# Folding a block-diagonal matrix into a projection by 32 by 32 tiles of the TensorE array

## The chip, the cores and the metric

The kernel runs on one core of one Trainium2 chip. The metric is the device time of one execution in microseconds (us). The kernel before takes 1632.44 us (median of 3 runs, 1632.38 to 1632.49). PE is the tensor engine's matmul stream, PEld its weight loads, DVE the vector engine, ACT the scalar engine, SP the queue that issues most transfers.

## The reference, cut to what matters

Four blocks run in turn on x of 2048 by 1024: attention, gated linear unit, and both again. Only attention is concerned:

```python
H = 32; Dh = D // H                       # 32 heads of 32
q, k, v = split(layernorm(x) @ wqkv)
phi = lambda t: jnp.where(t > 0, t + 1, jnp.exp(t)) + 1e-6
pq, pk = phi(q), phi(k)
kv  = einsum("bhsd,bhse->bhde", pk, v)    # one 32 by 32 matrix per head
num = einsum("bhqd,bhde->bhqe", pq, kv)
den = einsum("bhqd,bhd->bhq", pq, pk.sum(s)) + 1e-6
x = x + (num / den) @ wo
```

As (pq kv) wo = pq (kv wo), the kernel multiplies each head's 32 by 32 matrix into its 32 rows of wo once ("the fold", whose result is T) and then does one dense product per 128 tokens.

## The kernel before: the parts that matter

kv comes out as 128 by 128 blocks for four heads each. Only the four diagonal 32 by 32 pieces are wanted; a mask zeroes the others, and the fold is a full matmul per block and half of wo's columns:

```python
# head of the program: a mask with ones in the diagonal blocks, five memsets on DVE
for b in range(H):                                   # finish_kv: H = 2 here
    nc.vector.tensor_tensor(out=kvT[...], in0=kv[b]..., in1=self.mask..., op=ALU.mult)
...
def fold_wo(i):                                      # i = 0..15
    n2, g = divmod(i, G)
    ps = pool.tile([P, NW], F32, tag=tag)            # one of four PSUM banks
    nc.tensor.matmul(ps, lhsT=kvT[:, g, :], rhs=ring.get((l, f"o{n2}"))[:, g, :],
                     start=True, stop=True)
    # copied to T by ACT (odd g) or DVE (even g)
...
# two folds after each of eight units of eight matmuls
```

The head of the program issues ten warm-up matmuls on zeros, which wait for one DVE memset queued behind those of the mask.

## Time and profile before

| what | before | how to read it |
|---|---|---|
| time, median | 1632.44 us | device time of one execution |
| span of the profiled run | 1631.2 us | first to last instruction |
| PE busy | 1625.2 us | nearly all of the span |
| full folds | 32 | 16 in each of two attention layers |
| projections (L403) | 1024 | the order in which these read is changed too |

Busy times of PE rest on modelled ends of matmuls, so prices of matmuls below are taken from start to start where they can be; the length of a group in a timeline includes the modelled end of its last matmul. In the rows of a timeline the columns are start, length in us, engine, line, operation, output and inputs, shape, count, and in brackets idle time of the engine before it with what ended it.

### The profile page before, as it was taken

How to read it: one execution, taken by the hardware profiler on the slowest of the kernel's cores; microseconds unless marked ns; L12 is line 12 of the kernel's file. 1: busy time of each engine (PE TensorE's matmuls, PEld its weight loads, DVE VectorE, ACT ScalarE, POOL GpSimd, SP SyncE). 2: the span in 40 equal slices, each digit the busy share in tenths (PEclk: the TensorE clock that was granted, in tenths of full speed). 3: DMA queues.
4: the chain of work that ended last, by engine and by line, in shares of the span. 5: the costliest groups of instructions: out<-in, count | busy, mean ns of one | idle time of the engine just before them, and what ended most of it. 6: DMA issues, size and time to landing. Idle time of an engine off the chain costs nothing.

```text
span 1631.2 us, 18462 instructions
## 1 busy us (share of the span) xinstructions
PE 1625.2 (100%) x7658; PEld 743.1 (46%) x7658; DVE 570.8 (35%) x947; ACT 331.2 (20%) x636; POOL 201.5 (12%) x134
## 2 busy tenths in 40 slices
PE   9999999999999999999999999999999999999999
PEld 4444444444444444444444444444444444444444
DVE  7855695113212222222264547941022111211211
ACT  6741212101110110111066312121011101101110
POOL 2349220000000000000023592100000000000000
PEclk9999999999999999999999999999999999999999
DMA  8313637448445445544550147464554454454452
GB/s 248 62 52 59 175 71 201 145 151 232 155 145 188 160 150 162 168 151 138 166 124 1 52 98 244 84 193 145 179 166 149 156 186 155 145 165 155 155 161 72
DMA packets 298245, 235.05 MB, mean 144 GB/s; under 512 B 101296, under 2 KB 294192, under 8 KB 298160
## 3 DMA queue, kind: packets, MB, share of 16 engines
q1 hardware_dynamic: 292832, 228.75, 47.5%
q10 hardware_dynamic: 5328, 5.11, 0.9%
q8 instruction: 60, 0.98, 0.2%
q14 instruction: 25, 0.20, 0.0%
HBM read 201.33 MB, written 8.39 MB: 129 GB/s over the span
## 4 chain that ended last, share of the span: by engine, by line
PE 98%; ACT 1%; DMA 0%; DVE 0%; issue 0%; SPq 0%
PE pu L628 24%; PE pg L628 24%; PE acc L652 23%; PE ps L403 12%; PE ps L520 7%; PE ps L437 7%; DMA t<-in_A_wqkv_dram 0%; PE kv L450 0%; PE fold L508 0%; PE acc_last L652 0%; ACT e L355 0%; ACT e L354 0%; ACT e L356 0%; PE tp L264 0%; DVE pq L362 0%
## 5 line engine op out<-in xcount | busy, mean ns | idle before, releaser
L628 PEld LDWEIGHTS <-t 128*128 128x128 bf16 x3584 | 350.7, 98 | 422.8
L628 PE MATMUL pu<-xnT,t 128*128 128x512 bf16 x1792 | 423.3, 379 | 0.0
L628 PE MATMUL pg<-xnT,t 128*128 128x512 bf16 x1792 | 423.3, 379 | 0.0
L652 PE MATMUL acc<-t,hT 128*128 128x512 bf16 x1764 | 382.5, 379 | 0.0
L634 DVE TENSOR_TENSOR hT<-pu,rg 128x512 bf16<-128x512 f32 x224 | 154.6, 690 | 572.9 <-PE pu L628 572.9
L633 ACT ACTIVATE rg<-pg 128x512 f32<-128x512 f32 x224 | 133.5, 596 | 737.4 <-PE pg L628 737.4
L652 PEld LDWEIGHTS <-hT 128*128 128x128 bf16 x1820 | 178.1, 98 | 209.0
L403 PE MATMUL ps<-t,xnT 128*128 128x512 bf16 x1024 | 224.7, 379 | 1.0 <-DMA t<-in_A_wqkv_dram 0.6
L403 PEld LDWEIGHTS <-xnT 128*128 128x128 bf16 x1024 | 99.8, 98 | 121.2 <-issue 1.8
L520 PE MATMUL ps<-T,pqT 128*128 128x512 bf16 x512 | 111.8, 379 | 0.0
L149 ACT ACTIVATE rstd<-mv,eps 128x1 f32<-128x1 f32 x64 | 18.7, 293 | 327.8 <-DVE mv L147 327.7
L669 DVE TENSOR_TENSOR xo<-x,acc 128x512 bf16<-128x512 f32 x31 | 21.3, 688 | 170.3 <-PE acc L652 170.3
L483 POOL TENSOR_TENSOR prod<-pq,zrow 128x1024 f32<-128x1024 bf16 x32 | 67.9, 2123 | 87.8 <-DVE den L488 75.6
L142 DVE BATCH_NORM_STATS2 stats<-x 128x6 f32<-128x512 f32 (+1 forms) x120 | 77.9, 672 | 0.8
L520 PEld LDWEIGHTS <-pqT 128*128 128x128 bf16 x512 | 50.1, 98 | 60.4
L417 POOL CAST ksum<-x 128x512 f32<-128x512 bf16 x2 | 1.7, 866 | 605.4 <-DVE x L362 605.4
L666 DVE TENSOR_TENSOR x<-x,acc 128x512 f32<-128x512 f32 x32 | 21.6, 674 | 138.5 <-PE acc L652 137.4
L419 POOL TENSOR_TENSOR ksum<-ksum,slab 128x512 f32<-128x512 f32 x46 | 53.6, 1171 | 86.3 <-DVE slab L362 76.8
L362 DVE SCALAR_TENSOR_TENSOR pq<-ps,e 128x512 bf16<-128x512 f32 x64 | 44.0, 688 | 55.7 <-ACT e L356 55.2
L495 POOL TENSOR_TENSOR pq<-pq,den 128x1024 bf16<-128x1024 bf16 x32 | 61.7, 1933 | 3.1 <-DVE den L490 3.1
L488 DVE TENSOR_REDUCE den<-prod 128x32 f32<-128x1024 f32 x32 | 38.9, 1217 | 52.6 <-POOL prod L483 52.6
L437 PE MATMUL ps<-slab,x 128*128 128x512 bf16 x256 | 56.6, 379 | 0.0
(58 smaller groups left out, 609.0 us busy)
## 6 DMA issues: line engine op xcount, KB each, us to landing
t<-in_B_W_gate_dram SPq DMA_DIRECT2D x56, 1024.0 KB, 7.0
t<-in_B_W_up_dram SPq DMA_DIRECT2D x56, 1024.0 KB, 5.4
t<-in_B_W_down_dram SPq DMA_DIRECT2D x64, 896.0 KB, 5.0
t<-in_A_wqkv_dram SPq DMA_DIRECT2D x11, 1024.0 KB, 6.2
t<-in_A_wo_dram SPq DMA_DIRECT2D x4, 1024.0 KB, 6.8
away<-x SPq DMA_DIRECT2D x8, 512.0 KB, 4.1
x<-away SPq DMA_DIRECT2D x8, 512.0 KB, 7.8
out_dram<-xo ACTq DMA_DIRECT2D x31, 128.0 KB, 2.3
```

Source lines behind the costliest of these rows:

```text
L142: self.nc.vector.bn_stats(out=stats[:, c, :], in_=src[:, c * fmax:(c + 1) * fmax])
L362: nc.vector.scalar_tensor_tensor(out=out, in0=ps, scalar=0.0, in1=e, op0=ALU.max, op1=ALU.add)
L403: nc.tensor.matmul(ps, lhsT=self.xnT[l, l_q][:, kt, j * P:(j + 1) * P], rhs=w[:, kt, :], start=(kt == 0), stop=(kt == KT - 1))
L419: nc.gpsimd.tensor_tensor(out=ksum[:, cols], in0=ksum[:, cols], in1=pk, op=ALU.add)
L437: nc.tensor.matmul(ps, lhsT=self.xn[l, t][:, d * P:(d + 1) * P], rhs=self.pk[l, t][:, h * NW:(h + 1) * NW], start=(t == 0), stop=(t == sel ...
L483: nc.gpsimd.tensor_tensor(out=prod, in0=pq_of[sc, j], in1=zrow, op=ALU.mult)
L495: nc.gpsimd.tensor_tensor(out=heads(pq), in0=heads(pq), in1=den[:, :].unsqueeze(2).to_broadcast([P, D // HD, HD]), op=ALU.mult)
L520: nc.tensor.matmul(ps, lhsT=pqT[sc][:, g, j * P:(j + 1) * P], rhs=T[g // 2][:, g % 2, n2 * NW:(n2 + 1) * NW], start=(g == 0), stop=(g == G ...
L628: nc.tensor.matmul(ps, lhsT=w[:, kt, fi * P:(fi + 1) * P], rhs=self.xnT[l, q][:, kt, :], start=(kt == 0), stop=(kt == KT - 1))
L633: nc.scalar.activation(out=rg, in_=pg, func=ACT.Relu)
L634: nc.vector.tensor_tensor(out=h[:, fi, :], in0=pu, in1=rg, op=ALU.mult)
L652: nc.tensor.matmul(ps[:, 0:n], lhsT=hT[ft // 4][:, ft % 4, j * P:(j + 1) * P], rhs=wd[:, k, i * n:(i + 1) * n], start=(ft == 0), stop=(ft ...
```

## The change

The intent is to spend no array rows on zeros. Each head's 32 by 32 matrix becomes the weights of one tile of the array, so sixteen heads fill it. For this, sixteen heads need sixteen different places (row group by column group), so the heads of keys and queries are put in another order when the projection reads its weights. The mask goes away. The diff, cut to its core:

```diff
-        self.mask = ...                       # and its five memsets
+        R = P // HD
+        by_row = lambda a: a.rearrange("p (i b d) -> p i b d", i=R, d=HD)
 # projections of k and q
-    nc.tensor.matmul(ps, lhsT=..., rhs=w[:, kt, :], ...)
+    nc.tensor.matmul(by_row(ps), lhsT=..., rhs=w[:, kt, :].rearrange("p (b i d) -> p i b d", ...), ...)
 # kv
-    rhs=mt[:, g * P:(g + 1) * P]
+    rhs=by_row(mt[:, b * NW:(b + 1) * NW])[:, :, i, :]
 # finish_kv: two masked products on DVE
+    nc.vector.tensor_copy(out=kvT[first half], in_=kv[0])
+    nc.scalar.activation(out=kvT[second half], in_=kv[1], func=ACT.Copy)
 # fold: four bursts of sixteen tiles in place of sixteen full matmuls
+    for b in range(R):
+        g = a * R + b
+        for i in range(R):
+            e = slice(i * HD, (i + 1) * HD)
+            nc.tensor.matmul(ps[i][b * HD:(b + 1) * HD, :], lhsT=kvT[e, g, e],
+                             rhs=wo[e, g, :], start=True, stop=True,
+                             tile_position=(i * HD, b * HD))
 # a burst after every second unit, starting one unit earlier
```

More of the change, by code (lines that the diff above doesn't have):

```diff
@@ L124, in __init__ @@
         nc.vector.memset(self.ones, 1.0)
-        self.mask = self.const.tile([P, P], F32, name="mask")
-        nc.vector.memset(self.mask, 0.0)
-        for i in range(P // HD):
-            nc.vector.memset(self.mask[i * HD:(i + 1) * HD, i * HD:(i + 1) * HD], 1.0)
         self.eps6 = self.const.tile([P, 1], F32, name="eps6")
@@ L402, in project @@
                     between()
-                nc.tensor.matmul(ps, lhsT=self.xnT[l, l_q][:, kt, j * P:(j + 1) * P],
-                                 rhs=w[:, kt, :], start=(kt == 0), stop=(kt == KT - 1))
+                nc.tensor.matmul(by_row(ps), lhsT=self.xnT[l, l_q][:, kt, j * P:(j + 1) * P],
+                                 rhs=w[:, kt, :].rearrange("p (b i d) -> p i b d", i=R, d=HD),
+                                 start=(kt == 0), stop=(kt == KT - 1))
             return ps
@@ L449, in kv_step @@
                 b, i = divmod(g, NW // P)
-                nc.tensor.matmul(kv[b][:, i * P:(i + 1) * P],
+                nc.tensor.matmul(kv[b][:, i * P:(i + 1) * P].rearrange("p (i d) -> p i d", d=HD),
                                  lhsT=ring.get((l, f"v{b}"))[:, d, i * P:(i + 1) * P],
-                                 rhs=mt[:, g * P:(g + 1) * P], start=(d == 0 and i == 0),
+                                 rhs=by_row(mt[:, b * NW:(b + 1) * NW])[:, :, i, :], start=(d == 0 and i == 0),
                                  stop=(d == KT - 1 and i == NW // P - 1),
@@ L460, in finish_kv @@
             n = NW // P
-            for b in range(H):
-                nc.vector.tensor_tensor(out=kvT[:, b * n:(b + 1) * n, :],
-                                        in0=kv[b][:, :].rearrange("p (g e) -> p g e", e=P),
-                                        in1=self.mask[:, :].unsqueeze(1).to_broadcast([P, n, P]),
-                                        op=ALU.mult)
+            nc.vector.tensor_copy(out=kvT[:, 0:n, :].rearrange("p g e -> p (g e)"), in_=kv[0])
+            nc.scalar.activation(out=kvT[:, n:2 * n, :].rearrange("p g e -> p (g e)"), in_=kv[1],
+                                 func=ACT.Copy)
         def q_unit(sc, j, c, lag=None):
@@ L500, in z_scale, with fold_wo @@
             nc.sync.dma_start_transpose(out=pqT[sc][:, :, j * P:(j + 1) * P], in_=pq)
-        def fold_wo(i):
-            n2, g = divmod(i, G)
-            if n2 == 0 and g % 2 == 0:
-                T.append(self.slab.tile([P, 2, D], BF16, tag="slab", name=f"T{l}_{g // 2}"))
-            pool, tag = (self.kvp, f"kv{g // 2 % 2}") if g % 2 else (self.ps3, "b")
-            ps = pool.tile([P, NW], F32, tag=tag, name=f"fold{l}_{i}")
-            nc.tensor.matmul(ps, lhsT=kvT[:, g, :], rhs=ring.get((l, f"o{n2}"))[:, g, :],
-                             start=True, stop=True)
-            dst = T[g // 2][:, g % 2, n2 * NW:(n2 + 1) * NW]
-            if g % 2:
-                nc.scalar.activation(out=dst, in_=ps, func=ACT.Copy)
-            else:
-                nc.vector.tensor_copy(out=dst, in_=ps)
+        def fold_wo(n):
+            n2, a = divmod(n, H)
+            if n2 == 0:
+                T.extend(self.slab.tile([P, 2, D], BF16, tag="slab", name=f"T{l}_{2 * a + i}")
+                         for i in range(2))
+            ps = [pool.tile([P, NW], F32, tag=tag, name=f"fold{l}_{n}_{i}") for i, (pool, tag) in
+                  enumerate(((self.kvp, "kv0"), (self.kvp, "kv1"), (self.ps3, "b"), (self.ps3, "b")))]
+            wo = ring.get((l, f"o{n2}"))
+            for b in range(R):
[5 more added lines that the diff above has]
+                                     tile_position=(i * HD, b * HD))
+            for i in range(R):
+                g = a * R + i
+                dst = T[g // 2][:, g % 2, n2 * NW:(n2 + 1) * NW]
+                if g % 2:
+                    nc.scalar.activation(out=dst, in_=ps[i], func=ACT.Copy)
+                else:
+                    nc.vector.tensor_copy(out=dst, in_=ps[i])
         def out_unit(sc, j, n2):
@@ L585, in with_fold @@
             def with_fold(u, i):
-                return lambda: (u(), fold_wo(2 * i), fold_wo(2 * i + 1))
-            run(q3[:3])
-            run([with_fold(u, i) for i, u in enumerate(q3[3:] + out0[:3])])
+                return lambda: (u(), fold_wo(i // 2) if i % 2 == 0 else None)
+            run(q3[:2])
+            run([with_fold(u, i) for i, u in enumerate(q3[2:] + out0[:1])])
+            run(out0[1:3])
             ring.free_slowly((l, "o0"), later, 2)
```

## The prediction

> **What bounds the kernel now.** I read the page first: busy shares, then the chain that ended last. It says that the tensor engine is the whole story.
>
> ```profile
> PE 1625.2 (100%) x7658; PEld 743.1 (46%) x7658; DVE 570.8 (35%) x947; ACT 331.2 (20%) x636; POOL 201.5 (12%) x134
> PE 98%; ACT 1%; DMA 0%; DVE 0%; issue 0%; SPq 0%
> PE pu L628 24%; PE pg L628 24%; PE acc L652 23%; PE ps L403 12%; PE ps L520 7%; PE ps L437 7%; DMA t<-in_A_wqkv_dram 0%; PE kv L450 0%; PE fold L508 0%; PE acc_last L652 0%; ACT e L355 0%; ACT e L354 0%; ACT e L356 0%; PE tp L264 0%; DVE pq L362 0%
> ```
>
> PE is busy for 1625.2 of 1631.2 us and holds 98% of the chain. So only two things move the time: PE's own work, and a wait that the change makes PE take. Work on DVE, ACT or the queues is free as long as PE does not stand for it. The fold is under half a per cent of the chain, so a large move could only come from something else that the change touches.
>
> Next the view of the tile that the change rewrites (the fold), with its count and durations, and the page's row of the projections, whose addressing is changed as well:
>
> ```profile
> L508 PE MATMUL fold<-t,kvT x32: 379/379/380, 173.6 to 997.6; 128*128 128x512 bf16 x32
> L512 ACT ACTIVATE T<-fold x16: 592/592/597, 174.4 to 998.0; 128x512 bf16<-128x512 f32 x16
> L514 DVE CAST T<-fold x16: 678/681/684, 175.6 to 998.2; 128x512 bf16<-128x512 f32 x16
> L403 PE MATMUL ps<-t,xnT 128*128 128x512 bf16 x1024 | 224.7, 379 | 1.0 <-DMA t<-in_A_wqkv_dram 0.6
> ```
>
> Then the timeline of the first attention layer where keys-times-values ends and folding begins (start, length, engine, line, what, count):
>
> ```profile
> 167.98 0.61 PE L450 MATMUL kv<-mt,t 128*128 128x128 bf16 x8
> 168.40 0.37 SPq L35 DMA_DIRECT2D t<-in_A_wo_dram  x1
> 168.43 5.34 PE L403 MATMUL ps<-t,xnT 128*128 128x512 bf16 x24
> 169.94 1.28 DVE L462 TENSOR_TENSOR kvT<-kv,mask 128x512 bf16<-128x512 f32 x2
> 173.61 0.59 PE L508 MATMUL fold<-t,kvT 128*128 128x512 bf16 x2
> 174.04 1.89 PE L403 MATMUL ps<-t,xnT 128*128 128x512 bf16 x8
> 174.50 0.43 DVE L360 TENSOR_SCALAR e<-e 128x512 f32<-128x512 f32 x1 [0.57 <-ACT e L352]
> 174.96 0.69 DVE L362 SCALAR_TENSOR_TENSOR pq<-ps,e 128x512 bf16<-128x512 f32 x1
> 175.57 0.68 DVE L514 CAST T<-fold 128x512 bf16<-128x512 f32 x1
> ```
>
> The reader is to see the price of one matmul in a stream. Eight of 512 columns span 1.89 us with a last one of 0.379, so they follow each other every (1.89 - 0.379)/7 = 0.216 us, and some 0.163 us of each is a tail that the next one hides. Two folds take 174.04 - 173.61 = 0.43 us, again 0.216 each. Pairs of weight load and 128-column matmul follow each other every (0.61 - 0.219)/7 = 0.056 us. No PE row has idle time before it here: today the fold costs PE just its streaming.
>
> **What the Trainium skill says.** (1) "TensorEngine Tiling (Array Packing)", Key Properties: different tiles can load weights and multiply in parallel, but changing the tiling mode drains the engine. The kernel before has only the full mode, so its trace can't confirm either. (2) "TensorE: Matmul & The Clock Gate", Measured speedup vs the span model: sixteen 32 by 32 tiles of 512 columns ran 10.6 times faster than one after the other, and the span is modelled as one matmul's duration plus about 4 ns per further tile. No run here shows it yet. The section before it, The mechanism, adds that a weight load passes ahead of matmuls in flight only where its row group differs, or with the background weights. (3) "SBUF — State Buffer", the note on cachelines in Door 1: strides are free as long as consecutive accesses stay in a 16-byte line. The projections will now read runs of 32 bf16, 64 bytes, or four whole lines. All streamed operands before are contiguous, so the trace has no counterexample.
>
> **The change part by part.**
>
> *Removed.* 16 full folds per attention layer, 32 in all: 32 x 0.216 = 6.9 us of PE on the path. They spend 128 rows on blocks that the mask has made three quarters zero. Also two masked evictions per layer on DVE (0.64 us each), and a few memsets in the head, which delay nothing but warm-up matmuls.
>
> *Added.* The order of instructions shows 64 tile matmuls per layer, each with its own weight load, in four bursts of sixteen; 192 more rows of the PE list in all (2 x 96 matmul-and-load pairs more than now). Each burst has the sixteen positions of the array once and replaces four full folds, 4 x 0.216 = 0.863 us. What a burst costs is the whole question. With the page's span model on this trace's 379 ns: 0.379 + 15 x 0.004 = 0.439 us. If the engine drains on entering the mode, the 0.163 us tail of the projection before is no longer hidden, and the burst's own tail isn't either: 0.163 + 0.439 = 0.60 us from the end of one stream to the start of the next. Saving 0.26 us per burst, eight bursts: 2.1 us. If no drain shows, the burst costs 0.439 - 0.163 = 0.276 us and eight save 4.7 us, the most that can be had. If weight loads and matmuls go out no faster than the 0.056 us per pair seen above, a burst takes 16 x 0.056 = 0.90 us plus two tails of 0.163, 1.22 us, and eight lose 2.9 us. The order within a burst (four row groups, then the next column group) speaks for an early start of three loads of every four, so I lean to the middle case but not all the way: estimate -1.9 us.
>
> *Moved: the reading order.* 1024 projections and 128 kv matmuls read their streamed operand in runs of 32. The page gives no cost for it; PSUM is still written contiguously. I take 0 as most likely. One lost array cycle per run (about 0.42 ns, from 0.216 us / 512) would be 16 x 0.42 = 6.7 ns per projection, 6.9 us in all.
>
> *Moved: the evictions.* They are 16 per layer as before, but now four at once, and the next burst needs all four banks (it starts over in the same two kv banks and two others). Between bursts there are two projections, 2 x 1.73 = 3.45 us, and the burst. DVE has there two joins of 0.43 + 0.69 and two casts of 0.68: 3.6 us, in a period of some 4.0. ACT has two exponentials of 0.60 and two copies of 0.59: 2.4 us. Walking the first layer: projections end at 171.9 (two units after kv, one sooner than today), the kv copies are out by 170.6 (DVE from 169.94, 0.68; ACT beside it), the burst ends about 172.5, DVE is done with its joins at 173.9 and with the casts at 175.3, and the second burst starts at 176.0. So 0.7 us of room. The same step gives the third burst at 180.0 and its banks free at 179.2, and the fourth at 184.1 with banks free at 183.3. Wo's second half is issued at 168.40, and wo loads take 8.1 us at the longest, so it's there by 176.5, before 180.0; in the second attention layer issue is at 977.03 and use at about 988.6. I expect no new PE wait.
>
> *Sum.* 1632.4 - 1.9 + 0 + a little for the skew of the risks = 1630.8 us.
>
> **The rivals.**
> 1. *The tiles do not run beside each other* (weight loads of one row group wait for matmuls in it): then up to 64 x 0.216 = 13.8 us per layer in place of 3.5, or +20.7 us: 1653, still within 2%. For it: the rule on row groups in the second page. Against it: the same page's 10.6 times. A milder form, four row groups together but the column groups in turn, gives 4 x 0.216 per burst plus drains of 0.33 and about 1635.
> 2. *The reading order slows the streamed operand.* With one cycle per run, 1637 to 1639; at half rate, 1152 matmuls would add up to 228 us, 1855, the only way that I see to "slower". Against it: whole 16-byte lines.
> 3. *Eviction becomes the bound of the fold.* DVE is at 3.6 of 4.0 us there. If the bursts are short, the period shrinks to about 3.73 and the room to under 0.5 us, but the next burst just waits for what is left: at most some tenths of a us each, 1 to 2 us in all. It would eat the gain, not more.
>
> **Range and chances.** The three cases of a burst give 1627.7, 1630.3 and 1635.3; runs of before differ by 0.1 us only, so the range is that of the mechanism: 1627.5 to 1636.0. Faster by 2% is 32.6 us, and all folds together are 6.9: 0.005. Slower by 2% takes rival 2 in its strong form: 0.03. The rest, 0.965, is within 2%.
>
> **What would show it right or wrong.** Right: PE's group of folds has 128 matmuls, and from the end of the projection's stream before a burst to the start of the next projection there are 0.45 to 0.75 us; projections still step by 0.216 us (their group's mean 379 ns, eight in 1.89 us); no PE wait on a cast or copy of T. Wrong: a burst of over 0.9 us (then issue or drain decides), a projection group with a mean over 385 ns, or PE idle time before folds released by DVE.

## The result, and the profile after

The changed kernel took 1629.86 us (median of 4 runs, 1629.42 to 1630.68) beside 1632.47 us for the kernel before: 2.6 us, or 0.16%, less. A ratio in this document is the mean time of one kernel's fast runs over that of the other's of the same rounds, so it is not quite the ratio of the medians. Here it is 0.9985 (95% interval 0.9967 to 1.0002). In all fourteen runs of this kernel the median is 1630.41 and the range 1629.16 to 1630.87. The interval includes 1, but every one of these runs is under every run of the kernel before (1632.24 us or more).

First the page's busy shares and chain by engine, after:

```profile
PE 1621.7 (100%) x7754; PEld 739.3 (45%) x7754; DVE 566.7 (35%) x940; ACT 331.8 (20%) x638; POOL 201.9 (12%) x134
PE 98%; ACT 1%; DVE 1%; DMA 1%; issue 0%; SPq 0%; DVEq 0%
```

PE still sets the end; it has 96 more matmuls and yet 3.5 us less busy time. Next the view of the fold's tile, and the page's row of the projections:

```profile
L515 PE MATMUL fold<-t,kvT x128: 383/385/386, 172.8 to 991.7; 32*32 32x512 bf16 x128
L522 ACT ACTIVATE T<-fold x16: 592/594/605, 173.5 to 992.7; 128x512 bf16<-128x512 f32 x16
L524 DVE CAST T<-fold x16: 680/682/685, 174.7 to 993.1; 128x512 bf16<-128x512 f32 x16
L404 PE MATMUL ps<-t,xnT 128*128 128x512 bf16 x1024 | 224.3, 380 | 2.2 <-DMA t<-in_A_wqkv_dram 1.7
```

There are 128 tile matmuls, each as long as a full one (385 against 379 ns), so all the gain must come from running beside each other. The evictions cost what they did. The projections keep their 224 us, but 1.7 us of waiting for their first weights stands beside them where it was 0.6. The timeline of the first attention layer around the first two bursts:

```profile
168.81 0.61 PE L452 MATMUL kv<-mt,t 128*128 128x128 bf16 x8
169.25 3.62 PE L404 MATMUL ps<-t,xnT 128*128 128x512 bf16 x16
170.84 0.68 DVE L463 CAST kvT<-kv 128x512 bf16<-128x512 f32 x1
172.80 0.14 PEld L515 LDWEIGHTS <-kvT 32*32 32x32 bf16 x16 [0.42 <-issue]
172.80 0.43 PE L515 MATMUL fold<-t,kvT 32*32 32x512 bf16 x16
173.17 3.63 PE L404 MATMUL ps<-t,xnT 128*128 128x512 bf16 x16
174.74 1.28 DVE L524 CAST T<-fold 128x512 bf16<-128x512 f32 x2
176.73 0.43 PE L515 MATMUL fold<-t,kvT 32*32 32x512 bf16 x16
```

Sixteen weight loads take 0.14 us together, and sixteen matmuls 0.43 us from the first start to the last end, so they start (0.43 - 0.385)/15 = 3 ns apart. The stream of the projections before ends at 169.25 + 16 x 0.216 = 172.71. The burst therefore begins 0.09 us after it; its last stream ends near 172.80 + 0.045 + 0.216 = 173.06, and the next projection starts 0.11 us later. From stream end to stream start that is 0.46 us in place of 0.863 for four full folds. DVE has emptied its banks at 176.02, 0.7 us before the next burst needs them.

To price the whole fold stage I use two fixed marks of the second attention layer in each kernel: the first matmul on a slab tile and the first matmul of the gated unit that follows. Before, then after:

```profile
917.80 1.89 PE L437 MATMUL ps<-slab 128*128 128x512 bf16 x8
1047.85 1.89 PE L628 MATMUL pg<-xnT,t 128*128 128x512 bf16 x8
```

```profile
917.06 1.89 PE L439 MATMUL ps<-slab 128*128 128x512 bf16 x8
1045.54 1.89 PE L639 MATMUL pg<-xnT,t 128*128 128x512 bf16 x8
```

The stage takes 130.05 us before and 128.48 us after: 1.57 us less for four bursts, 0.39 us each. The same reading in the first layer gives 131.78 and 130.21, again 1.57. So the fold gave 3.14 us, but the span went from 1631.2 to 1628.9, 2.3 less. The rest, 0.83 us, was lost before the first mark of the first layer, at the start of the program. Two lines of each timeline show it, the first wait for weights and that mark. Before, then after:

```profile
9.48 0.59 PE L403 MATMUL ps<-t,xnT 128*128 128x512 bf16 x2 [0.58 <-DMA t<-in_A_wqkv_dram]
107.44 8.80 PE L437 MATMUL ps<-slab,x 128*128 128x512 bf16 x40
```

```profile
10.23 0.59 PE L404 MATMUL ps<-t,xnT 128*128 128x512 bf16 x2 [1.73 <-DMA t<-in_A_wqkv_dram]
108.27 8.80 PE L439 MATMUL ps<-slab,x 128*128 128x512 bf16 x40
```

The loss was not expected, and half of the experiments are about it. The figure of 0.83 belongs to these two executions: the profiled one of the kernel before took 1632.99 us, 0.55 more than its median, and in b_fours below, which has the same head, the mark is at 106.89. Against that the changed kernel's profile lost 1.4 us.

### The profile page after: what moved, and what is told of

It reads as the page before. It is cut to its first block, busy times and chain, and to the rows that moved or that the text cites. A ratio compares the mean times of both kernels' runs of the same rounds, so it can differ in the third digit from the quotient of the medians.

```text
span 1628.9 us, 18772 instructions
## 1 busy us (share of the span) xinstructions
PE 1621.7 (100%) x7754; PEld 739.3 (45%) x7754; DVE 566.7 (35%) x940; ACT 331.8 (20%) x638; POOL 201.9 (12%) x134
## 4 chain that ended last, share of the span: by engine, by line
PE 98%; ACT 1%; DVE 1%; DMA 1%; issue 0%; SPq 0%; DVEq 0%
PE pu L639 24%; PE pg L639 24%; PE acc L663 23%; PE ps L404 12%; PE ps L530 7%; PE ps L439 7%; DMA t<-in_A_wqkv_dram 1%; PE kv L452 0%; PE acc_last L663 0%; ACT e L351 0%; ACT e L350 0%; PE fold L515 0%; DVE st L138 0%; ACT e L352 0%; DVE slab L358 0%
```

## The experiments

The first theory: inside the tile mode, tiles at different places stream together, sixteen for the price of one stream; going into the mode and out of it costs some 0.2 us per burst; reading order and schedule are free. Its rivals: issue sets the pace, the gain comes from schedule or small tiles as such, or the reading order costs something. The second theory, on the head: without the mask's memsets the warm-up starts earlier, and that makes the start of the program slower in some runs. Its rival is chance.

The stage of the second layer between the two marks, in every profile, is the cleanest number. The right column is the difference from the changed kernel over four bursts:

| kernel | stage, us | per burst against after |
|---|---|---|
| before | 130.05 | +0.39 |
| after | 128.48 | 0 |
| a_rows | 128.48 | 0 |
| a_double | 129.35 | +0.22 |
| a_split | 130.16 | +0.42 |
| a_diag | 130.91 | +0.61 |
| b_fours | 130.05 | +0.39 |
| b_order | 130.05 | +0.39 |

**a_double: every burst twice.** Edit to the changed kernel; the result stays right.

```diff
-            for b in range(R):
+            for b in [*range(R), *range(R)]:
```

> The changed kernel with every burst's sixteen tiles issued twice in a row, the second time over the same results (still right). From the trace, a burst of 0.465 us is 0.216 of streaming, 15 steps of 3 ns and about 0.2 us of gaps on going into the tile mode and out of it. Theory (streams set the pace inside the mode, gaps are paid once per burst): 16 further tiles cost 0.22 to 0.27 us, so 8 x 0.25 = 2.0 us more than the changed kernel. Rival (issue of loads and matmuls at 0.056 us per pair sets the pace): 16 x 0.056 = 0.9 us per burst, 7.2 us more. Rival (a tile waits for the tail of the tile before it at its own place): 0.385 us per burst, 3.1 us more.

It took 1631.11 us (median of 4, 1630.99 to 1632.06; before 1632.48). Its timeline in the first layer:

```profile
171.49 0.65 PE L515 MATMUL fold<-t,kvT 32*32 32x512 bf16 x32
172.08 3.63 PE L404 MATMUL ps<-t,xnT 128*128 128x512 bf16 x16
```

32 tiles end 0.65 us after the first start, where 16 end after 0.43; in the trace the second sixteen start 0.226 us after the first. Sixteen tiles more cost 0.22 us per burst in the stage: one stream of 0.216. Issue at 0.056 us per pair and waiting for tails are both out.

**a_split: two halves of eight, two projection matmuls between them.** The same tiles, twice the visits to the mode.

```diff
-                return lambda: (u(), fold_wo(i // 2) if i % 2 == 0 else None)
+                    tiles, evict = fold_wo(i // 2)
+                    u(lambda: tiles((0, 1)))     # before the unit's last two matmuls
+                    tiles((2, 3))
+                    evict()
```

> The changed kernel with every burst in two halves of eight tiles, two full projection matmuls between them: the same tiles, twice the changes of mode. Theory: each half costs one stream and the two gaps, 0.216 + 7 x 0.003 + 0.2 = 0.44 us, so two halves 0.88 in place of 0.465: 8 x 0.41 = 3.3 us more, which is as slow as full folds (1632.5 or so). If the gaps came with the first tiles only and not with the change of mode, it would be 8 x 0.22 = 1.8 us more. No new PE wait expected, as banks are free about 0.7 us ahead.

It took 1633.07 us (median of 4, 1632.53 to 1633.86). Two half-bursts:

```profile
171.50 0.41 PE L516 MATMUL fold<-t,kvT 32*32 32x512 bf16 x8
171.84 0.60 PE L404 MATMUL ps<-t,xnT 128*128 128x512 bf16 x2
172.37 0.41 PE L516 MATMUL fold<-t,kvT 32*32 32x512 bf16 x8
172.71 3.20 PE L404 MATMUL ps<-t,xnT 128*128 128x512 bf16 x14
```

A second visit costs 0.42 us per burst: 0.216 for its stream and 0.20 for its gaps. As expected, this eats the whole gain: eight tiles per visit do no better than full matmuls.

**a_diag: tiles without places of their own.** Natural order of heads, each head on the diagonal place that it has there.

```diff
-                nc.tensor.matmul(by_row(ps), ...)        # and the other reorderings
+                nc.tensor.matmul(ps, ...)
-                    nc.tensor.matmul(ps[i][b * HD:(b + 1) * HD, :], ..., tile_position=(i * HD, b * HD))
+                    nc.tensor.matmul(ps[h][e, :], ..., tile_position=(i * HD, i * HD))
```

> The changed kernel without the new order of heads: tiles of 32 by 32 too, sixteen to a burst, but each head on the tile of the array's diagonal that its natural place gives it, so that four tiles share each of four places and twelve places stay empty (result right). Theory (a tile needs a place of its own to run beside the others): four streams in turn, 4 x 0.216 + 0.25 = 1.1 us per burst, so 8 x 0.65 = 5.2 us more than the changed kernel, about 1635. Rival (small tiles are quicker by themselves, wherever they lie): 0.47 to 0.6 us per burst, 1629.5 to 1631.

It took 1634.52 us (median of 4, 1634.11 to 1635.38), right results:

```profile
172.64 1.04 PE L516 MATMUL fold<-t,kvT 32*32 32x512 bf16 x16
173.84 3.40 PE L404 MATMUL ps<-t,xnT 128*128 128x512 bf16 x15 [0.16 <-issue]
```

A burst is 1.04 us long and costs 0.61 us more than the changed kernel's, 0.22 more than four full folds. In the trace its tiles start in fours, at 0, 0.226, 0.442 and 0.657 us: four streams in turn. Small tiles are not quicker as such; the places of their own are the change's whole gain, and that is what the order of heads buys.

**a_rows: the loops over row and column groups exchanged.**

```diff
-            for b in range(R):
-                for i in range(R):
+            for i in range(R):
+                for b in range(R):
```

> The changed kernel with the two loops of a burst exchanged, so that the four tiles of one row group come one after the other in place of one tile of each row group in turn. Theory (each tile loads and streams in a place of its own, so order does not matter): the burst stays at 0.46 to 0.47 us, its loads within 0.14 us, time as the changed kernel's, 1629.2 to 1630.9. Rival (a weight load waits for matmuls in flight in its row group): loads of three of every four tiles come only after a stream of 0.216 us, so a burst of four streams, 1.1 us, 5 us more in all.

It took 1629.67 us (median of 4, 1629.31 to 1630.57). Loads and burst are the same to the last digit, so neighbours in one row group do not wait for each other:

```profile
171.55 0.14 PEld L515 LDWEIGHTS <-kvT 32*32 32x32 bf16 x16 [0.42 <-issue]
171.55 0.43 PE L515 MATMUL fold<-t,kvT 32*32 32x512 bf16 x16
```

**b_fours: the schedule alone.** The kernel before with full folds in fours, at the changed kernel's places and in its banks.

```diff
-                return lambda: (u(), fold_wo(2 * i), fold_wo(2 * i + 1))
+                return lambda: (u(), fold_wo(i // 2) if i % 2 == 0 else None)   # four full folds each
```

> The kernel before with its full masked folds issued four at a time, at the places and with the four banks of the changed kernel: the change's schedule without its tiles. Theory (the gain is the tiles'): 1632.4 to 1632.6 us. Rival (part of the gain is the earlier and bunched schedule): 1631 to 1632. If the evictions held the banks too long, PE would show waits on them and the time would be over 1632.6.

It took 1632.51 us (median of 4) beside 1632.48, and its stage is that of the kernel before. Nothing of the gain is the schedule's. The move of one kv eviction from DVE to ACT was not run alone; the views of the fold's tile show no wait of PE before a fold in either kernel.

**b_order: the reading order alone**, on the kernel before. Its result is wrong (relative error 0.24), as the folds are left in the old order.

```diff
-                nc.tensor.matmul(ps, lhsT=..., rhs=w[:, kt, :], ...)
+                nc.tensor.matmul(by_row(ps), lhsT=..., rhs=w[:, kt, :].rearrange("p (b i d) -> p i b d", ...), ...)
```

> The kernel before with the changed kernel's reading order alone (projections and kv read their streamed operand in runs of 32), full folds, and therefore a wrong result on purpose. Theory: the order is free: 1632.4 to 1632.6 us, projections 379 to 380 ns. Rival: one array cycle per run of 32: 16 x 0.42 ns x 1024 = 6.9 us more, 1639; or a tenth of that, 0.7 us more, still outside the scatter of before.

It took 1632.46 us (median of 5) beside 1632.51 us, ratio 1.0000. The row of its projections:

```profile
L406 PE MATMUL ps<-t,xnT 128*128 128x512 bf16 x1024 | 224.4, 379 | 0.4 <-ACT xnT L271 0.3
```

The stage between the marks holds only 64 of the second layer's 512 projections. The stretch before it, from the first matmul of the first gated unit to the first mark of the second layer, holds the other 448, and it takes 678.58 us in both kernels (239.22 to 917.80 before, 238.62 to 917.20 here). Runs of 32 elements are free for this streamed operand: a tenth of a cycle per run would be 0.3 us in that stretch alone.

**The head: a_again, a_mask, b_early, and later a_warm, a_mask2, a_again2.** a_again and a_again2 are the changed kernel unedited, a_mask and a_mask2 have the dead memsets back. b_early is the kernel before with the mask's memsets behind the one that the warm-up waits for. a_warm has 14 warm-up matmuls.

```diff
 # a_mask, a_mask2 (changed kernel)
+        self.mask = ...; nc.vector.memset(...)      # the five of before, read by nothing
 # b_early (kernel before)
-        nc.vector.memset(self.mask, ...)            # five memsets, ahead of
         nc.vector.memset(zero, 0.0)
+        nc.vector.memset(self.mask, ...)            # now after
 # a_warm (changed kernel)
-        for _ in range(10):
+        for _ in range(14):
```

> The changed kernel once more, unedited, beside the other three of this call. Its fold should show the same burst (0.46 to 0.47 us from stream end to next stream) and a time of 1629.3 to 1630.8 us; its runs are expected to scatter by about 1 us, where the kernel before scatters by 0.1 us. If the scatter was an accident of the first four runs, all five agree within 0.3 us.

> The changed kernel with the five mask memsets put back into the head, where nothing reads them. Theory: their removal lets the warm-up matmuls start at 1.34 in place of 2.10 us, and something about that earlier start makes the first weights land later (10.23 against 9.48 us) in some runs; the fold alone is worth 8 x 0.39 = 3.1 us. Then this kernel is at 1632.45 - 3.1 = 1629.3 us with a scatter of 0.1 to 0.2 us, and its first weights land near 9.5 us. Rival: the late landing is chance or comes from elsewhere in the program; then this kernel scatters as the changed kernel does, 1629.4 to 1630.7.

> The kernel before, with the mask's memsets moved behind the one that the warm-up matmuls wait for, so that the warm-up starts at about 1.3 us as in the changed kernel; the fold is untouched. Theory of the early warm-up: slower than before by 0 to 1.2 us and scattering, as the head of the changed kernel does. Rival (chance, or another cause): 1632.4 to 1632.5 us like the kernel before.

> The changed kernel with 14 warm-up matmuls in place of 10, still starting at about 1.34 us, so that no idle stretch is left between the warm-up and the first transposes near 6.4 us. Theory (the idle stretch of 0.6 to 1.8 us after an early warm-up is what lets the granted clock fall to half in some runs): none of the half-speed projections at 8 to 10 us that a_again, b_early and a_diag showed (six in 2.7 us in place of 1.6), time 1629.3 to 1629.7 us, scatter 0.3 us. Rival (the early start itself, or chance): half-speed projections in the profile or runs up to 1630.9 again.

> The changed kernel with the dead memsets once more, for the head question: theory 1629.4 to 1629.6 us with at most one run in five above 1630; rival (chance) the same spread as the unedited changed kernel of this call.

> The changed kernel unedited, for the comparison within this call: 1629.2 to 1630.9 us as in its nine runs so far; theory of the head: about half of the runs above 1630.

| kernel | warm-up starts, us | runs | median, us | range, us |
|---|---|---|---|---|
| a_again | 1.35 | 5 | 1630.41 | 1629.16 to 1630.87 |
| a_again2 | 1.35 | 5 | 1630.49 | 1629.22 to 1630.77 |
| a_mask | 2.10 | 5 | 1629.50 | 1629.38 to 1630.31 |
| a_mask2 | 2.10 | 5 | 1629.45 | 1629.30 to 1629.76 |
| a_warm | 1.34 | 5 | 1629.71 | 1629.28 to 1629.85 |
| b_early | 1.34 | 5 | 1633.48 | 1632.51 to 1633.79 |

With the first four runs, nine of fourteen runs of the unedited changed kernel are above 1630 us, and one of the fifteen of a_mask, a_mask2 and a_warm. b_early is slower than the kernel before (median 1632.51) by about the same 1 us, with the fold untouched. So about 1 us is lost in most runs where the warm-up starts early and nothing fills the time behind it; a_warm starts as early and loses nothing. The kernel before has stragglers of its own, though: of the nine runs in that call three were at 1633.0 to 1633.2, and one of nine in the last call at 1635.81.

The start of PE's timeline in the kernel before, then in a_again, then in a_warm:

```profile
2.10 4.45 PE L224 MATMUL idle<-zero 128*128 128x512 bf16 x10 [2.10 <-DVE zero L221]
6.34 1.06 PE L264 MATMUL tp<-ident,x 128*128 128x128 bf16 x8
7.66 1.24 PE L403 MATMUL ps<-t,xnT 128*128 128x512 bf16 x4 [0.26 <-ACT xnT L271]
```

```profile
1.35 3.81 PE L220 MATMUL idle<-zero 128*128 128x512 bf16 x10 [1.35 <-DVE zero L217]
6.90 0.72 PE L260 MATMUL tp<-ident,x 128*128 128x128 bf16 x8 [1.75 <-DVE x L154]
7.99 2.74 PE L404 MATMUL ps<-t,xnT 128*128 128x512 bf16 x6 [0.37 <-ACT xnT L267]
```

```profile
1.34 5.30 PE L220 MATMUL idle<-zero 128*128 128x512 bf16 x14 [1.34 <-DVE zero L217]
6.47 0.61 PE L260 MATMUL tp<-ident,x 128*128 128x128 bf16 x8
7.55 1.04 PE L404 MATMUL ps<-t,xnT 128*128 128x512 bf16 x4 [0.47 <-ACT xnT L267]
```

Before, the warm-up reaches the first transposes. In a_again it ends early and PE idles 1.75 us; the first six projections then take 2.74 us, and in the trace they start 0.40 to 0.43 us apart, twice 0.216. The view by stretches of time has the granted clock at 0.50 there (stretch, span, busy time and count of PE, PEld, DVE, ACT, POOL, then the clock, DMA share and GB/s):

```profile
8.00:10.00 2.00, 2.00 (x5) 0.72 (x6) 1.04 (x4) 0.50 (x2) 0.00 (x0) 0.50 1.08 354
```

In a_warm the idle stretch is filled and the projections run at full speed. Six projections at half speed are also in the profiles of b_early (2.69 us) and a_diag (2.74 us), both with the early warm-up. No profile with a late or filled warm-up has them; there at most the first projection is slow.

The three are not the same event, though. The starts of single matmuls in the traces show that the warm-up begins at half speed in every profile, 0.43 us from one to the next. In a_again it reached full speed at 4.4 us and fell back from 7.78 to 11.19 us, by the trace's clock records. In b_early and a_diag no fall is seen: all of the warm-up and the first transposes ran at half speed, and full speed came first at 10.4 and 10.7 us, where the first clock record of each stands. (The view by stretches gives 1.00 for 8 to 10 us there, but the trace has no clock record for that time, and the steps of 0.40 to 0.43 us speak against it.) In all other profiles full speed came by about 8.1 us at the latest. So in two of the three the early warm-up ended before it had brought the clock up. What sets the moment within an execution is not shown: a_double, a_rows, a_split and a_again2 ran at full speed after idle stretches of 0.85 to 1.22 us, while b_early and a_diag idled for only 0.78 and 0.84 us.

The first profile of the changed kernel lost its time in another way: its projections ran at full speed but waited until 10.23 us for weights. What made those weights late is open. They came at 9.48 us in the kernel before and at 8.93 us in b_fours, both with the late warm-up, so they scatter without an early one too. a_mask's expectation that the late landing is the whole loss fell, as three later profiles show half-speed matmuls instead. Which of these the runs without a profile had is not known.

The best is the changed kernel with its old head, a_mask: 1629.50 and 1629.45 us. That beats both kernels, the changed one by about 1 us of median within each call.

## Why the prediction was right, point by point

The time was predicted at 1630.8 us in a range of 1627.5 to 1636.0, and "within 2%" at 0.965. It came out at 1629.86.

- **PE bounds, and only its own work or a new wait counts: right.** The new wait that did appear was in the head, not where it was looked for.
- **The skill's span model: right.** 0.439 us was worked out for a burst's matmuls, 0.43 measured. a_double bears it out without a modelled end: sixteen further tiles cost one stream.
- **The cost of changing the mode: mis-sized.** The middle case had two tails of 0.163 us exposed and a burst at 0.60 us, with eight saving 2.1 us, and the estimate leaned back to -1.9. The gaps measured 0.09 and 0.11 us, and a_split's second visit cost 0.20 us beyond its stream, so a burst costs about 0.47 us and the fold gave 3.14 us, not 1.9. The room stated beforehand, 0.45 to 0.75, held it, near its edge.
- **The reading order at zero: right,** by b_order. The rival of one cycle per run fell.
- **The walk through the evictions: right.** 0.7 us of room was worked out before the second burst and 0.71 measured. No PE wait on a bank or on wo appeared.
- **"A few memsets in the head, which delay nothing but warm-up matmuls": this step failed.** It saw what the memsets delay but not that the delay was of use. Removing them cost from nothing to about 1.4 us per run (median of the changed kernel against a_mask: 0.9 to 1.0 us in the two shared calls). This hid part of the larger gain of the fold, so the median came closer to the prediction than its two terms were. That is luck: the fold gave 1.24 us more than estimated, and a loss that was not foreseen took part of it back.
- **The rival of serial tiles: wrong for this order of heads.** a_diag shows that it is right where tiles share a place.
- **Slips that moved nothing.** The tiles add 96 pairs of load and matmul, which are the 192 rows; "2 x 96 pairs" counts them twice. The 228 us of rival 2 lead to 1860 us, not 1855. And "runs of before differ by 0.1 us only" held for the first runs: later ones lie from 1632.24 to 1633.23 us, with one at 1635.81.

## What to carry to other kernels

As measured here, small tiles of the array pay only when tiles at different places run in one visit to the tile mode: count the places filled, charge per visit one stream, some 3 ns for each further tile and about 0.2 us, and compare that with the full matmuls replaced. The four streams replaced here leave 0.39 us of gain per visit; with eight tiles per visit nothing was left. And an instruction removed ahead of a warm-up moves the warm-up: look at what fills the time until the first real work, and at the moment when full speed is first granted, before calling the removal free.

## What the Trainium skill lacked or had wrong

- "TensorEngine Tiling (Array Packing)", Key Properties: it says that a change of mode drains the engine, without a cost. Here a visit to the 32 by 32 mode costs 0.20 us beyond its streams (a_split), less than the two exposed tails of 0.163 us that I took for it.
- "TensorE: Matmul & The Clock Gate", The mechanism: its rule that loads pass ahead only where the row group differs (or with background weights) sets no price here: sixteen loads take 0.14 us in either order of the loops, also where four in a row share a row group (a_rows).
- The same page, Measured speedup vs the span model: the model fits (0.43 us against 0.439), but it prices one visit. Further tiles within the visit cost a sixteenth of a stream each (0.22 us per sixteen, a_double), and tiles at one place go one after the other (1.04 us per sixteen on four places, a_diag); the section gives neither number.
- "SBUF — State Buffer", Door 1, the note on cachelines: it gives no figure for a streamed matmul operand in short runs. Runs of 64 bytes are free: a stretch with 448 such projections takes 678.58 us with and without them (b_order).
- "TensorE: Matmul & The Clock Gate", Part 1: its table of the two states puts the fall to half speed at an idle window of some 3.4 us. In a_again the longest idle stretch was 1.75 us, followed by transposes and another 0.37 us of waiting, and the clock record is 0.50 from 7.78 to 11.19 us. The part also tells of falls through frequent short idle times, but gives no length for them.
